# Eight attention steps with their division by the row sum moved behind the values product

## The chip, the cores and the metric

The kernel runs on one core of one Trainium2 chip. The metric is the device time of one execution in microseconds (us), the median of three runs. The engines are TensorE (PE in the profile, PEld for its weight loads), VectorE (DVE), ScalarE (ACT), GpSimd (POOL) and SyncE (SP), which here issues nearly all DMAs. Each engine works through its own instructions in the order in which the program emits them, as the rows of the trace below show it; engines wait for one another by semaphores.

## The reference

Attention over 8 batches, 8 heads, 576 tokens and a head width of 64, in float32, with a threshold on the scores; its output is rearranged to 4608 tokens of width 512 and goes through a two-layer feed-forward block with ELU.

```python
scores = (q @ k.T) / sqrt(64)
thresh = max(scores) - tau
scores = where(scores >= thresh, scores, -1e9) - max(scores)
attn = exp(scores)
attn = attn / (sum(attn) + 1e-9)
o = attn @ v                      # (8, 8, 576, 64)
x = o.transpose(0, 2, 1, 3).reshape(4608, 512)
h = x @ w_in                      # (4608, 2048)
g = where(h > 0, h, exp(min(h, 0)) - 1)
out = g @ w_out                   # (4608, 512)
```

## The kernel before, in words

The unit of attention is a *pair*: two heads of one batch, so 4 pairs for each of 8 batches. A pair has five *steps*, one for each tile of 128 query tokens (tiles 0 to 3) and one for the last 64 tokens of both heads. The list `steps` sets their order. It begins with tiles 0 and 1 of pairs 0, 1, 2, 3; these are steps 0 to 7, step n being tile n % 2 of pair n // 2. Tiles 2, 3 and the tail of batch 0 are steps 8 to 19, and the later batches follow.

A step holds 128 query rows in the partitions and 576 keys for each of two heads along the free axis. Its jobs, all made in `early_tasks`, are named here as in the code, with "n/h" for step and head:

- `sc`: TensorE writes the scores into PSUM (L673). `max` (VectorE, L730) takes the row maximum, `th` the threshold.
- `exp` and `mask`: either ScalarE's exponential (L768) and VectorE's compare-and-multiply (L775), or two activations on ScalarE (L753, L759), write the weights `w`, with their row sums accumulated beside them.
- `su` and `rec`: the sum and its reciprocal `rs`, 128x2 (L783 or L720, and L789).
- `norm` n/h: `w` is multiplied by `rs`, 128x576 for each head, on GpSimd (L726), ScalarE (L714) or VectorE (L709), as the tables ACT_NORM and NORM_DVE say. In steps 0 to 7 eleven of the sixteen are on GpSimd, four on ScalarE, one (4/0) on VectorE.
- `part` n/x and `put` n/x, x from 0 to 2: TensorE turns 4, 4 and 1 blocks of 128x128 of `w` into a PSUM tile `rt` (L792), and ScalarE, or VectorE where PUT_DVE says so, copies it to the tile `wTa` or `wTb` (L808).
- `val` (pair, part): TensorE multiplies the values by the turned weights of two steps, into a PSUM tile `pv` (L925 and L930, 18 recorded instructions). `out` (pair, part): the result, 128 channels by 256 tokens, is copied to `xt`, the input of the feed-forward block (L1060).

The PSUM tiles `rt` and `pv` share one pool of two buffers, `psum["t"]`. `room_for("t", release)` keeps a list of two releases: before a third tile is taken, the oldest one's release (its `put` or `out`) is emitted.

Beside the steps the first 60 us hold the conversion of the feed-forward weights from their stored form, in pieces of 128x512: `rest` (L485 or L505), `shift` (L492 or L494), `add` (L500, GpSimd), `sign` (L510, ScalarE) and `end` (L518, VectorE). Pairs are prepared by `prep` (VectorE, L577 and L590), `scale` (L582 or L584) and `copy` (GpSimd, L629).

The order of all this is written by hand: each job has a due time, shifted by the table MOVED; jobs are emitted by due time, and `do` emits what a job needs ahead of it.

```python
def do(x):
    job = made[x]
    if not job[4]:
        job[4] = True
        for y in job[3]:
            if y:
                do(y)
        job[2]()
...
def room_for(pool, release):
    while len(taken[pool]) >= 2:
        taken[pool].popleft()()
    taken[pool].append(release)
```

From step 10 on (after `switch`, at some 50 us) the feed-forward block of earlier tokens is woven in between the steps.

Of the kernel before, what the change touches and what calls it, by code (L numbers as in the profile page):

```python
# [10 lines left out]
FP32 = mybir.dt.float32  # L11
# [4 lines left out]
ALU = mybir.AluOpType  # L16
# [352 lines left out]
def kernel(  # L369
# [10 lines left out]
    nc = tc.nc  # L380
    PSUM = bass.MemoryType.PSUM
    P = 128
    B, H, S, D = q.shape
    DM, DF = moe_w_in.shape
    NC = S // P
    MAIN = NC * P
# [5 lines left out]
    KJ = DM // P  # L392
    NFT = DF // P
    NPAIR = H // 2
# [8 lines left out]
    xpool = ctx.enter_context(tc.tile_pool(name="xpool", bufs=2))  # L403
# [13 lines left out]
    wstage = early.enter_context(tc.tile_pool(name="wstage", bufs=2))  # L417
    wpool = [wstage]
    banks = ExitStack()
    psum = {"t": banks.enter_context(tc.tile_pool(name="ps_t", bufs=2, space=PSUM))}  # L420
# [214 lines left out]
    wTs, xts, open_steps, turns = {}, {}, {}, {}  # L635
# [80 lines left out]
    def total_act(pr, i, hs):  # L716
# [2 lines left out]
        st["summed"] = True  # L719
        nc.scalar.activation(st["su"][:, cs], st["sm"][:, cs, 0], AF.Identity, bias=st["sm"][:, 0, 1:2])  # L720

    def normalize(pr, i, hs):
        st = open_steps[pr, i]
        for h in hs:
            wv = st["w"][:, h * S : (h + 1) * S]
            nc.gpsimd.tensor_scalar(wv, wv, st["rs"][:, h : h + 1], 1.0, ALU.mult, ALU.mult)  # L726
# [64 lines left out]
    def transpose(dst, src):  # L791
        nc.tensor.matmul(dst, src, idents[-1], is_transpose=True, skip_group_check=True)  # L792
# [104 lines left out]
    def fetch(pr, i):  # L897
# [11 lines left out]
        else:  # L909
# [2 lines left out]
                back.rearrange("k (a b) n -> k a b n", b=2),  # L912
            )

    def values(pr, part, pv=None):
        b, j = divmod(pr, NPAIR)
        vm, vd = (raws[pr][x] for x in ("vm", "vd"))
        wT = wTs.pop((pr, part))
        if b not in xts:
            xts[b] = xpool.tile([P, KJ, MAIN], FP32, name="xt")  # L920
        n = wT.shape[1] * T
        if pv is None:
            pv = psum["t"].tile([P, 512], FP32, name="pv", tag="rt")
        watch = on_banks if wide else lambda *a: None
        watch(nc.tensor.matmul(pv[:, :n], vd, wT[:, :, NC], start=True, stop=False, skip_group_check=True), pv[:, :n])  # L925
        for c in range(NC):
            for h in range(2):
                g0, g1 = (2 * h, 2 * h + 10) if part else (0, 2 * NT)
                o = pv[h * D : (h + 1) * D, g0 * T : g1 * T]
                watch(nc.tensor.matmul(o, vm[:, h, c], wT[:, g0:g1, h * (NC + 1) + c], start=False, stop=(c == NC - 1),  # L930
                                       skip_group_check=True), o)
        return lambda: values_out(pr, part, pv)

    wide, turned_by = [], []
# [120 lines left out]
    def values_out(pr, part, pv):  # L1055
        b, j = divmod(pr, NPAIR)
        q0, n = TAIL * part, (3 if part else 2) * NT * T
        watch = on_banks if wide else lambda *a: None
        o = pv[:, q0 : q0 + 2 * P]
        watch(nc.scalar.copy(xts[b][:, j, part * 2 * P : (part + 1) * 2 * P], o), o)  # L1060
        if part:
            xs = opool.tile([P, TAIL], FP32, name="xs", bufs=2)
            for h in range(2):
                r = slice(h * D, (h + 1) * D)
                o = pv[r, h * (n - TAIL) : h * (n - TAIL) + TAIL]
                watch(nc.scalar.copy(xs[r], o), o)  # L1066
            nc.sync.dma_start(xtail[j, :, b * TAIL : (b + 1) * TAIL], xs)
            pairs.pop(pr), raws.pop(pr)
# [106 lines left out]
    steps = [(pr, i) for pr in range(NP) for i in ((0, 1, NC, 2, 3) if pr >= JOINED else range(NB))]  # L1175
    steps[:per_seq] = [(pr, i) for x in ((0, 1), (2, 3, NC)) for pr in range(NPAIR) for i in x]
    LATE = 10

    def behind(pr, i):
        if i in (1, NB - 1):  # L1180
# [114 lines left out]
    def task(x, t, key, f, *needed):  # L1295
        each = "_".join(map(str, x)) if isinstance(x, tuple) else x
        made[x] = [t + (MOVED.get(key, 0.0) if key else 0.0) + MOVED.get(each, 0.0), len(made), f, needed, False]
# [10 lines that stand above are left out]
    def early_tasks():  # L1308
# [5 lines left out]
# [4 lines that stand above are left out]
# [54 lines left out]
        for pr in range(1, NPAIR + 6):  # L1372
            old = ("sc", number[pr - 2, NC]) if pr > 1 else None
            own = pr < NPAIR
            for x, name in enumerate("qk"):
                n = 2 * pr - 2 + x if own else number[pr - 1, 2 + x]
                k, late_ = kind(n), n >= LATE
# [26 lines left out]
                m = number[pr, 2] if own and not x else n  # L1404
# [15 lines left out]
        for i, (n, x) in enumerate(slots):  # L1420
            late_, k, t = n >= LATE, f"{kind(n)}{x}", begin[n]
            m, y = slots[max(i - 4, 0)]
# [47 lines left out]
        for n in range(MIDDLE):  # L1470
# [16 lines left out]
            for h in hs:  # L1487
                task(("max", n, h), at_(0.2 + 0.5 * h, 1.8 + 0.6 * h, 0.8 + 0.5 * h), f"max{h}{k}", lambda pr=pr, i=i, h=h: max_of(pr, i, h), ("sc", n))
                back = ("turned", n - (2 if last_ else WBUFS)) if n >= WBUFS else None
                t_exp, t_th, t_mask = (at_(0.3 + 0.7 * h, 2.0 + 0.6 * h, 1.0 + 0.5 * h), at_(0.4 + 0.7 * h, 2.2 + 0.6 * h, 1.1 + 0.5 * h),  # L1490
                                       at_(2.0 + 1.6 * h, 5.6 + 0.1 * h, 4.0 + 0.1 * h))
                if (n, h) in MASK_ACT:
                    task(("exp", n, h), t_exp, f"exp{h}{k}", lambda pr=pr, i=i, h=h: sink_of(pr, i, h), ("th", n, h), back, "late" if last_ else None)
                    task(("th", n, h), t_th, f"th{h}{k}", lambda pr=pr, i=i, h=h: pivot_of(pr, i, h), ("max", n, h))
                    task(("mask", n, h), t_mask, f"mask{h}{k}", lambda pr=pr, i=i, h=h: raise_of(pr, i, h), ("exp", n, h))
                else:
                    task(("exp", n, h), t_exp, f"exp{h}{k}", lambda pr=pr, i=i, h=h: exp_of(pr, i, h),
                         ("max", n, h), exps[-1] if exps else None, ("mask", *exps[-2][1:]) if len(exps) > 1 else None)
                    task(("th", n, h), t_th, f"th{h}{k}", lambda pr=pr, i=i, h=h: bound_of(pr, i, h), ("max", n, h))
                    exps.append(("exp", n, h))  # L1500
                    task(("mask", n, h), t_mask, f"mask{h}{k}", lambda pr=pr, i=i, h=h: mask_of(pr, i, h), ("exp", n, h), ("th", n, h),
                         ("mask", n, 0) if h and (n, 0) not in MASK_ACT else back, "late" if last_ else None)
                scaled = normalize_act if (n, h) in ACT_NORM else normalize_dve if (n, h) in NORM_DVE else normalize_pool
                norm = lambda pr=pr, i=i, h=h, f=scaled: f(pr, i, h)
                task(("norm", n, h), at_(5.0 + 0.8 * h, 6.2 + 0.1 * h, 5.4 + 0.1 * h), f"norm{h}{k}", norm, ("rec", n))
            task(("su", n), at_(3.8, 5.8, 4.4), f"su{k}", lambda pr=pr, i=i, hs=hs, f=total_act if n in SU_ACT else total_of: f(pr, i, hs), *[("mask", n, h) for h in hs])
            task(("rec", n), at_(3.8, 5.8, 4.4), f"rec{k}", lambda pr=pr, i=i, hs=hs: reciprocal_of(pr, i, hs), ("su", n))
# [10 lines left out]
            else:  # L1518
# [11 lines left out]
                m = n + 1  # L1530
# [14 lines left out]
            if i in (1, NC) and n < MIDDLE - 4:  # L1545
                got = []
                mine_ = [number[pr, x] for x in ((0, 1) if i == 1 else (2, 3, NC))]

                def run_values(pr=pr, part=part, got=got):
                    room_for("t", lambda: do(("out", pr, part)))  # L1550
                    got.append(values(pr, part))

                def run_out(pr=pr, part=part, got=got):
                    got[0]()
                    if (pr, part) == (NPAIR - 1, 0):
                        push_ffn(0)
                    elif (pr, part) == (NPAIR - 1, 1):
                        push_ffn(1)

                m = n + 2  # L1560
                t_val, t_out = (begin[m] + 4.0, begin[m] + 6.2) if m < LATE else (begin[m] + 0.4, begin[m] + 3.3)
                if n < per_seq:
                    t_val, t_out = begin[n + 1] + 4.2, begin[n + 2] + 1.5
                    if n >= LATE:
                        t_val, t_out = begin[n + 1] + 5.6, begin[n + 1] + 6.8
                elif any(m in SQUARES for m in mine_):
                    t_val, t_out = begin[n + 3] + 5.7, begin[n + 3] + 5.8
                elif SWITCH + 1 >= m >= SWITCH:
                    t_val, t_out = t_val - 8.0, t_out - 8.0
                task(("val", pr, part), t_val, f"val{k}", run_values, *[("landed", m) for m in mine_], ("v", pr))  # L1570
                task(("out", pr, part), t_out, f"out{k}", run_out, ("val", pr, part), ("out", pr, 0) if part else None)
            if n == 0:
                task("idle", t + 2.1, None, lambda: idle(16))
            if n >= SWITCH:
# [777 lines left out]
```

## Time and profile before

| what | value |
|---|---|
| median of three runs | 1259.22 us (1258.13 to 1260.99) |
| the profiled execution | 1259.32 us |
| its span in the profile | 1257.5 us |
| busy: PE, DVE, ACT, POOL | 99%, 83%, 51%, 58% of the span |
| granted TensorE clock | 1.00 |
| `norm` on GpSimd (L726) in the first 70 us | 14 of 798 ns |
| `norm` on ScalarE (L714) in the first 70 us | 8 of 773 ns |
| `out` (L1060) from `pv` | 16 of 365 ns |

The busy shares are averages over the whole span. The changed work lies in its first 50 us of 1257.5, where a step passes through all engines, so this stretch is read by itself: its busy time by engine, the chain of waits, and the timeline of each engine.

### The profile page before, as it was taken

Reading aid. Unit: us, or ns where it says so; the run is one execution under the profiler, and the core shown is the slowest. Engines: PE = TensorE matmul, PEld = TensorE weight load, DVE = VectorE, ACT = ScalarE, POOL = GpSimd, SP = SyncE. Lnnn points to the kernel's source line nnn. Section 1 sums busy time; section 2 is a strip of 40 time slices with the busy share of each in tenths; the row PEclk is TensorE's granted clock in tenths of the full one; section 3 lists DMA queues with packets and bytes.
Section 4 is the critical chain, followed back from the end, with each engine's and each line's share of the span. In section 5 each row is a group of like instructions: output and inputs, shape, how many; then the busy total and the mean of one; then the engine's idle time right before and its main releaser. Section 6 shows DMA issues by size and latency. Waiting matters only on the chain.

```text
span 1257.5 us, 21116 instructions
## 1 busy us (share of the span) xinstructions
PE 1243.9 (99%) x6598; PEld 957.0 (76%) x6598; DVE 1040.3 (83%) x2199; ACT 635.2 (51%) x1331; POOL 727.1 (58%) x1061
## 2 busy tenths in 40 slices
PE   8999999999999999999999999999999999999998
PEld 6676576467878787888778787878788887788886
DVE  7888778789798988898889879898889876776983
ACT  7989776664352526253534435252625353465330
POOL 4778655687475847666576747584766655122000
PEclk9999999999999999999999999999999999999999
DMA  7557688998889898998989998999889885000001
GB/s 134 151 177 177 177 244 234 260 248 216 239 239 266 245 240 224 241 263 228 252 206 253 237 231 231 256 257 240 228 238 262 221 241 175 20 1 1 1 34 34
DMA packets 325551, 245.74 MB, mean 195 GB/s; under 512 B 209216, under 2 KB 289984, under 8 KB 325440
## 3 DMA queue, kind: packets, MB, share of 16 engines
q1 hardware_dynamic: 323264, 243.65, 72.2%
q8 instruction: 52, 0.85, 0.3%
q10 hardware_dynamic: 2176, 0.75, 0.2%
q14 instruction: 59, 0.48, 0.1%
HBM read 154.53 MB, written 89.78 MB: 194 GB/s over the span
## 4 chain that ended last, share of the span: by engine, by line
PE 90%; DVE 3%; DMA 2%; ACT 2%; issue 1%; SPq 1%; POOL 1%; DVEq 0%; ACTq 0%; POOLq 0%
PE f L1678 23%; PE f L1818 22%; PE sc L977 8%; PE sc L1050 7%; PE f L2278 7%; PE f L2203 5%; PE f L1102 4%; PE sc L673 3%; PE f L1154 3%; PE f L2216 2%; PE pv L930 2%; PE rt L792 1%; PE sc L1042 1%; PE sc L1037 1%; DMA there<-x 1%
## 5 line engine op out<-in xcount | busy, mean ns | idle before, releaser
L984 DVE TENSOR_REDUCE mx<-sc 128x1 f32<-128x576 f32 x207 | 148.3, 750 | 28.5 <-PE sc L977 24.6
L726 POOL TENSOR_SCALAR w<-w,rs 128x576 f32<-128x576 f32 x144 | 115.8, 813 | 70.0 <-DVE rs L789 69.8
L1004 ACT ACTIVATE w<-sc,mx 128x576 f32<-128x576 f32 x113 | 81.5, 740 | 116.0 <-DVE mx L984 98.7
L868 DVE STREAM_TRANSPOSE x<-w 128x512 f32<-128x512 f32 (+1 forms) x153 | 108.9, 744 | 15.3 <-POOL w L726 11.3
L996 POOL TENSOR_SCALAR th<-mx,ntau 128x2 f32<-128x2 f32 (+1 forms) x114 | 33.8, 297 | 133.3 <-DVE mx L984 133.3
L977 PE MATMUL sc<-kT,qT 64*128 64x448 f32 (+4 forms) x736 | 103.4, 416 | 0.2 <-ACT xs L1066 0.2
L977 PEld LDWEIGHTS sc<-kT,qT 64*128 64x128 f32 x736 | 81.0, 186 | 25.1 <-issue 16.5
L1011 DVE SCALAR_TENSOR_TENSOR w<-sc,th,w 128x576 f32<-128x576 f32 x113 | 88.2, 811 | 9.4 <-ACT w L1004 9.2
L1678 PE MATMUL f<-xt,sw 128*128 128x256 f32 x384 | 93.8, 386 | 1.8 <-DVE g L1700 1.8
L1678 PE MATMUL f<-xt,w_in 128*128 128x256 f32 x384 | 92.2, 382 | 0.0
L1818 PE MATMUL f<-w_out,s 128*128 128x256 f32 x384 | 92.0, 382 | 0.1
L1818 PE MATMUL f<-w_out,g 128*128 128x256 f32 x384 | 92.0, 382 | 0.0
L1678 PE MATMUL f<-x,w_in 128*128 128x256 f32 x384 | 90.9, 379 | 0.0
L1818 PE MATMUL f<-t,s 128*128 128x256 f32 x384 | 90.8, 379 | 0.0
L726 POOL TENSOR_SCALAR e<-e,rs 128x576 f32<-128x576 f32 x91 | 67.1, 741 | 35.6 <-DVE rs L789 34.2
L1678 PEld LDWEIGHTS f<-xt,sw 128*128 128x128 f32 x384 | 69.4, 189 | 18.6 <-issue 4.8
L1678 PEld LDWEIGHTS f<-xt,w_in 128*128 128x128 f32 x384 | 71.7, 190 | 12.7 <-ACT w L1692 2.2
L1818 PEld LDWEIGHTS f<-w_out,g 128*128 128x128 f32 x384 | 72.0, 190 | 12.4 <-issue 3.1
L1818 PEld LDWEIGHTS f<-w_out,s 128*128 128x128 f32 x384 | 71.9, 190 | 12.4 <-issue 2.5
L1678 PEld LDWEIGHTS f<-x,w_in 128*128 128x128 f32 x384 | 72.8, 190 | 10.5 <-ACT s L1692 0.6
L1818 PEld LDWEIGHTS f<-t,s 128*128 128x128 f32 x384 | 72.8, 190 | 10.3 <-POOL s L1765 0.4
L1765 POOL TENSOR_TENSOR s<-g 128x256 f32<-128x256 f32 x96 | 74.9, 785 | 7.9 <-DVE g L1728 7.5
(316 smaller groups left out, 3103.5 us busy)
## 6 DMA issues: line engine op xcount, KB each, us to landing
there<-x SPq DMA_DIRECT2D x444, 144.0 KB, 3.5
wTb<-there SPq DMA_DIRECT2D x58, 576.0 KB, 6.5
wTa<-there SPq DMA_DIRECT2D x53, 576.0 KB, 5.0
sw<-win_sums SPq DMA_DIRECT2D x46, 384.0 KB, 4.9
t<-wout_sums SPq DMA_DIRECT2D x33, 512.0 KB, 6.2
qm<-in_q_dram SPq DMA_DIRECT2D x124, 72.0 KB, 4.9
wst<-in_moe_w_in_dram SPq DMA_DIRECT2D x16, 512.0 KB, 4.4
vm<-in_v_dram SPq DMA_DIRECT2D x64, 128.0 KB, 3.9
```

Source lines behind the costliest of these rows:

```text
L726: nc.gpsimd.tensor_scalar(wv, wv, st["rs"][:, h : h + 1], 1.0, ALU.mult, ALU.mult)
L868: nc.vector.transpose(x[:, :, c0 : c0 + nc_], src.rearrange("p (c g n) -> p g c n", c=nc_, n=T))
L977: on_banks(nc.tensor.matmul(o, qT[r, i * P : (i + 1) * P], kT[r, k0 : k0 + n], start=True, stop=True, skip_group_check=True), o)
L984: on_banks(nc.vector.tensor_reduce(st["mx"][:, h : h + 1], st["sc", h], axis=AX.XY if i == NC else AX.X, op=ALU.max, negate=True), st["sc" ...
L1004: on_banks(nc.scalar.activation(st["e", h], st["sc", h], AF.Exp, bias=st["mx"][:, h : h + 1]), st["sc", h])
L1011: on_banks(nc.vector.scalar_tensor_tensor(st["e", h], st["sc", h], st["th"][:, h : h + 1], st["e", h], ALU.is_ge, ALU.mult, accum_out=st[" ...
L1050: on_banks(nc.tensor.matmul(o, vm[:, h, c], parts[part][:, g0:g1, h * (NC + 1) + c], start=False, stop=(c == NC - 1), skip_group_check=Tru ...
L1678: nc.tensor.matmul(loc["banks"][place], left[:, j], right[:, j], start=(begins and j == 0), stop=(j == 1), skip_group_check=True)
L1765: engine.tensor_tensor(o, x, y, op)
L1818: nc.tensor.matmul(place(m), lhs, rhs, start=(begins and v == 0), stop=(v == RU - 1), skip_group_check=True)
L2203: nc.tensor.matmul(o, w.rearrange("p (j f) -> p j f", j=KJ)[:, j], m, start=(j == 0 and x == 0), stop=(j == KJ - 1 and x == 1), skip_group ...
L2278: nc.tensor.matmul(banks8[2 * i + x // 2], h[:, tok], w, start=(f == 0 and x != 1), stop=(f == NFT - 1 and x != 0), skip_group_check=True)
```

## The change

For steps 0 to 7 (tiles 0 and 1 of pairs 0 to 3) the weights are turned and multiplied by the values without having been divided by their row sums; the division is made on the product. As the product has channels in its partitions and tokens along the free axis, the factors have to be turned too:

- `norm` n/0 becomes `widen`: GpSimd writes `rs` (128x2) 64 times side by side, a 128x128 tile for both heads. `norm` n/1 becomes nothing. So 16 multiplications of 128x576 go, and 8 copies of 128x128 come.
- `spread` (pair): TensorE turns the two wide tiles of a pair into a PSUM tile `rt` from `psum["t"]`. It is needed by `val` (pair, 0), so it is emitted just ahead of it.
- `scales` (pair): ScalarE copies that, 128x256, to the place in `xt` where the values of this pair will stand. It is emitted when `room_for` calls for its release, or by `out` at the latest.
- `out` (pair, 0) for these pairs: instead of ScalarE's copy VectorE multiplies `pv` by what stands in `xt`, into `xt`.

The new jobs have a due time of 9000, so their place in the order follows from who needs them. Nothing else in the tables is altered.

```diff
+    def widen(pr, i):
+        st = open_steps[pr, i]
+        st["wide"] = wstage.tile([P, 2, D], FP32, name="rsd", bufs=3)
+        nc.gpsimd.tensor_copy(st["wide"], st["rs"].unsqueeze(2).broadcast_to([P, 2, D]))
...
+    def spread(pr):
+        rt = psum["t"].tile([P, 512], FP32, name="rt", tag="rt")
+        for i in range(2):
+            transpose(rt[:, i * P : (i + 1) * P], open_steps[pr, i]["wide"].rearrange("p h d -> p (h d)"))
+        return rt
+
+    def keep_spread(pr, rt):
+        b, j = divmod(pr, NPAIR)
+        if b not in xts:
+            xts[b] = xpool.tile([P, KJ, MAIN], FP32, name="xt")
+        scales[pr] = xts[b][:, j, : 2 * P]
+        nc.scalar.copy(scales[pr], rt[:, : 2 * P])
...
-        watch(nc.scalar.copy(xts[b][:, j, part * 2 * P : (part + 1) * 2 * P], o), o)
+        if (pr, part) in UNSCALED:
+            nc.vector.tensor_tensor(xts[b][:, j, : 2 * P], o, scales.pop(pr), ALU.mult)
+        else:
+            watch(nc.scalar.copy(xts[b][:, j, part * 2 * P : (part + 1) * 2 * P], o), o)
...
+    UNSCALED, LAST = [(pr, 0) for pr in range(NPAIR)], 9000.0
...
+                if (pr, int(i >= 2)) in UNSCALED:
+                    norm = (lambda: None) if h else lambda pr=pr, i=i: widen(pr, i)
                 task(("norm", n, h), at_(5.0 + 0.8 * h, 6.2 + 0.1 * h, 5.4 + 0.1 * h), f"norm{h}{k}", norm, ("rec", n))
...
-                task(("val", pr, part), t_val, f"val{k}", run_values, *[("landed", m) for m in mine_], ("v", pr))
-                task(("out", pr, part), t_out, f"out{k}", run_out, ("val", pr, part), ("out", pr, 0) if part else None)
+                if (pr, part) in UNSCALED:
+                    got_spread = []
+
+                    def run_spread(pr=pr, got_spread=got_spread):
+                        room_for("t", lambda: do(("scales", pr)))
+                        got_spread.append(spread(pr))
+
+                    task(("spread", pr), LAST, None, run_spread, *[("rec", m) for m in mine_])
+                    task(("scales", pr), LAST, None, lambda pr=pr, got_spread=got_spread: keep_spread(pr, got_spread[0]),
+                         ("spread", pr), ("out", pr - 1, 0) if pr else None)
+                task(("val", pr, part), t_val, f"val{k}", run_values, *[("landed", m) for m in mine_], ("v", pr),
+                     ("spread", pr) if (pr, part) in UNSCALED else None)
+                task(("out", pr, part), t_out, f"out{k}", run_out, ("val", pr, part),
+                     ("out", pr, 0) if part else ("scales", pr) if (pr, 0) in UNSCALED else None)
```

More of the change, by code (lines that the diff above doesn't have):

```diff
@@ L913, in fetch @@
             )
+    scales = {}
+    def spread(pr):
[9 more added lines that the diff above has]
+        nc.scalar.copy(scales[pr], rt[:, : 2 * P])
     def values(pr, part, pv=None):
```

## The prediction, on record before the result

> **What bounds the kernel now.** The page first. TensorE is busy nearly throughout, but this is an average, and the change touches only the first 50 us. So the second view is the busy time of each engine in stretches of 10 us (columns: us of PE, PEld, DVE, ACT, POOL; clock; DMA).
>
> ```profile
> PE 1243.9 (99%) x6598; PEld 957.0 (76%) x6598; DVE 1040.3 (83%) x2199; ACT 635.2 (51%) x1331; POOL 727.1 (58%) x1061
> ```
>
> ```profile
> 10.00:20.00 10.00, 8.61 (x56) 6.06 (x54) 7.59 (x19) 9.86 (x20) 6.74 (x10) 1.00 0.83 163
> ...
> 30.00:40.00 10.00, 9.30 (x72) 6.22 (x73) 9.39 (x23) 8.77 (x17) 5.25 (x11) 1.00 0.87 223
> ```
>
> GpSimd has the most room here, VectorE and ScalarE little. No engine alone sets the pace: the third view, the chain of waits (start, us, what), hops from one to the next. From 62.8 us on it is nearly all TensorE, without gaps until 212 us, so what the first 63 us lose or gain is kept to the end, unless a later stall takes it up.
>
> ```profile
> 28.30 0.53 DVE w L709
> ...
> 29.59 0.43 PE pv L925 x2
> ...
> 32.49 1.22 PE sc L673 x8
> 33.71 0.75 DVE mx L730
> ...
> 34.54 0.62 ACT e L768
> ...
> 36.48 0.33 PE rt L792
> 36.80 1.17 PE sc L673 x8
> ```
>
> Of the sixteen multiplications that go, only two places lie on this chain: steps 0/0 and 0/1 on GpSimd (a piece of 1.33 us at 12.63) and step 4/0 on VectorE (0.53 us at 28.30, above). The rest of the chain is work that stays. The fourth view, the timeline around 33 us, shows what `out` of pair 1 releases:
>
> ```profile
> 33.19 0.39 ACT L1060 COPY xt<-pv 128x256 f32<-128x256 f32 x1
> ...
> 33.59 0.14 PEld L792 LDWEIGHTS rt<-ident,w 128*128 128x128 f32 x1 [0.39 <-ACT xt L1060]
> ...
> 33.69 1.42 DVE L730 TENSOR_REDUCE mx<-sc 128x1 f32<-128x576 f32 x2 [0.36 <-PE sc L673]
> ...
> 33.95 0.27 ACT L808 COPY wTa<-rt 128x128 f32<-128x128 f32 x1 [0.37 <-PE rt L792]
> 34.54 1.41 ACT L768 ACTIVATE e<-sc,mx 128x576 f32<-128x576 f32 x2 [0.32 <-DVE mx L730]
> ...
> 35.03 0.69 DVE L518 SCALAR_TENSOR_TENSOR w_in<-wtop,wst 128x512 f32<-128x512 f32 x1
> ```
>
> ScalarE's copy (L1060) frees a PSUM buffer; TensorE's `part` 4/2 waits for just that (the bracket), ScalarE's `put` 4/2 waits for `part` 4/2, and `exp` 6/0, on the chain, stands behind it in ScalarE's queue.
>
> **The change, part by part.** Durations are those of the profiled execution, 1259.32 us with a span of 1257.5; it lies 0.1 us above the median.
>
> Work as such: GpSimd loses 11 x 0.80 = 8.8 us and gains 8 widenings. No row shows one; the 64x64 copy (L629) takes 0.235 us, the 128x128 select that makes `ident` 0.29, the 128x576 multiplication 0.80. I take 0.3, the 128x128 row, with 0.24 and 0.80 as ends; GpSimd's idle time (4.75 us of 10 between 30 and 40) hides either. ScalarE loses 4 x 0.77 = 3.1 us; its four copies of 128x256 change place (0.365 us each, L1060). VectorE loses 0.52 and gains four multiplications of 128x256 with one operand in PSUM, 0.42 us each by L1700 (422 ns, same shape and places). TensorE gains 8 turns of 0.15 us (four take 0.59 to 0.63, L792). None of these sums decides; the places do. I followed the jobs in the order in which `do` emits them, which the trace bears out, engine by engine.
>
> *Pair 0 (to 25 us).* `widen` 0 in place of two multiplications lets GpSimd's `scale` of pair 1 (14.07) start some 0.7 us sooner, but `sc` 2 also needs the buffer that `mask` 1/0 on VectorE frees at 14.61 (`sc` 2 began at 14.87), so about 0.5 us is won. ScalarE loses `norm` 1/1 and keeps this lead to the `put`s at 18.8; then 0.3 us of turns go in ahead of `val` 0, VectorE's `out` 0 (0.42) pushes `mask` 3/1, and `sc` 4 waits for `mask` 3/0 as before (end 22.8). By `exp` 4/0 (25.44), where ScalarE sets the pace, I find no difference. Bounds: 0.5 us gained, 0.4 us lost. Taken: 0.
>
> *Pair 1, ahead of `val`.* `part` 4/0 no longer waits for `norm` 4/0: it starts at 28.5 instead of 28.96. But the turns take one of the two PSUM buffers, so `val` 1 now needs the buffer of `part` 4/0 itself, and hence its `put` (0.59, L808): 28.5 + 0.63 + 0.05 + 0.59 + 0.05 = 29.85 against 29.59. The turns run while that copy does. +0.26 us; bounds 0 and +0.5.
>
> *Pair 1, `out`.* This is the large one. `out` 1 keeps its place in the emitted order: `max` 6/0, `max` 6/1, `end` 0, `put` 4/1, `out` 1, `part` 4/2, `put` 4/2, `exp` 6/0, `mask` 6/0. On ScalarE it had nothing of these but `put` 4/1 ahead of it and ran at 33.19. On VectorE it stands behind both maxima, which need `sc` 6, and behind `end` 0. Those end at 35.72, with the 0.26 above at 35.98. Then `out` 1 to 36.40, `part` 4/2 (0.33) to 36.75, `put` 4/2 (0.27) to 37.03, and only then `exp` 6/0, before at 34.54: +2.49, of which 0.26 is counted already. Behind the waiting TensorE instruction stand nine idle turns and `part` 5/0 and 5/1 (2.2 us, done by 38.9, where `put` 5/0 then is, so no more is lost); behind ScalarE's, both exponentials. +2.23 us; bounds 1.8 (part of the 0.69 us of `end` 0 could run in VectorE's gap of 0.36 us before the maxima) and 2.6.
>
> *Pair 2.* The two turns go between `sc` 7 and `val` 2, both on the chain (36.80, 37.98), with their buffer long free: +0.30 us; bounds 0 and 0.4. `scales` 2 (0.36) ahead of `out` 2 (0.42) ahead of `max` 8/0 costs VectorE 0.6 us more than before, but `exp` 8/0 waits on ScalarE for `put` 6/0 anyway: +0.05; bounds 0 and 0.5.
>
> *Pair 3.* The turns run while TensorE waits for `put` 7/2 (0.35 us at 47.29): nothing. `scales` 3 goes into ScalarE's queue between `norm` 8/0 and `exp` 9/0 (47.44 and 48.44, both on the chain): +0.36; `out` 3 delays `mask` 9/0 by as much on the parallel branch to `su` 9, so the two don't add up. Bounds 0.1 and 0.6.
>
> Sum: 0 + 0.26 + 2.23 + 0.30 + 0.05 + 0.36 = 3.2 us. What is left up to 62.8 us is GpSimd's `norm` 9 (51.47) and, behind it in the same queues, the conversion of weights: no changed work, and it starts when `rec` 9 is done. So 1259.3 + 3.2 = 1262.5, or 1262.4 from the median. The terms' bounds together give 1260.7 to 1263.8; not all ends can fall together, and I take 1261.0 to 1264.0 as this case's own range.
>
> **The rivals.** *Taken up again (same).* GpSimd is freed of 3.7 us between 33 and 46 (steps 5 to 7), and the chain passes through its conversions at 54.39 (0.88, L505) and 55.34 (1.31, L500). If these could run ahead of `norm` 9, up to 2.2 us would come back: 1260.3. Against it: they stand behind `norm` 9 in GpSimd's queue. The same end would come from transfers after 212 us that the chain waits for (4.42 us for `vd` at 225.76), if they don't shift with the rest.
>
> *The division was the brake (faster).* If `out` 1 did get through on VectorE before `max` 6/0 (its gap there is 0.36 us, the multiplication 0.42), the big term is gone, and with it the 0.26. The pieces on the chain then count: 1.33 - 0.3 at step 0, 0.53 + 0.14 at step 4, and 2.2 at the conversions, less 0.7 for pairs 2 and 3: 1259.3 - 3.2 = 1256.1. It decides at one point: which comes first on VectorE, the first multiplication of pair 1 or L518 of piece 0. The order of emission speaks against it.
>
> *TensorE's clock (slower still).* Between `sc` 6 (end 34.0) and `part` 4/2 (36.4) TensorE would stand for 2.4 us, more than any stop between 12 and 60 us now. If the clock then halved for the 3.4 us after it, 1.7 us of work would be lost, of the 4 us on the chain from 36.48 to 40.48: 1264.1. For now the granted clock is 1.00 in every stretch, also at 8 to 10 us, where TensorE is busy for 0.88 of 2 us.
> The Trainium skill (TensorE: Matmul & The Clock Gate, Part 1) has the clock halved after an idle window of about 3.4 us, free-running; by that rule 2.4 us is too short. No trace here shows a fall of the clock inside the work.
>
> That the change fails to do what it says I leave at nothing: each new job is needed by one that must run.
>
> **How the numbers follow.** Forecast 0.62, taken up again 0.19, faster 0.12, clock 0.07. About 0.2% (2.5 us) is what a measurement of this kernel tells from no change; the forecast is only just over it, so a tenth of its chance (0.06) goes to "same". Slower: 0.56 + 0.07 = 0.63; same: 0.19 + 0.06 = 0.25; faster: 0.12. The range reaches down over the rival that ends near 1260 and up over the clock: 1258.5 to 1264.8, which leaves out the faster case and little else.
>
> **What would show it.** Right: VectorE's multiplication of pair 1 at about 36 us, right after L518; TensorE's single turn of step 4 ended by "DVE xt", after a stop of over 2 us; `exp` 6/0 at about 37.0, `sc` 7 at about 39.3, `sc` 8 at about 43.2; and the stretch that now begins with `sc` at 62.82 beginning near 66. The clock 1.00 throughout. Wrong: `exp` 6/0 within 1 us of 34.54, or a shift at 37 us that is smaller at 63 or at 300 us; then the queue orders, or the keeping of a delay, were read wrongly.

## The result, and the profile after

The changed kernel takes 1261.47 us (median; 1259.99 to 1262.39), beside 1259.14 us for the kernel before in the same session. The ratio is 1.0017 with an interval of 1.0010 to 1.0024: slower by 2.1 us (1.3 to 3.0) by that ratio. The prediction said 1262.4 us, slower, by 3.2 us. The sign and nearly the size were right; the road to them was not. The term that made up 2.23 of the 3.2 us did not occur at all.

The profiled execution takes 1261.05 us with a span of 1259.3, against 1259.32 and 1257.5 before. First the page's busy line, then the busy time by stretches (us of PE, PEld, DVE, ACT, POOL; clock; DMA), which answer to the ones shown of before.

```profile
PE 1245.9 (99%) x6606; PEld 958.5 (76%) x6606; DVE 1041.9 (83%) x2202; ACT 633.4 (50%) x1327; POOL 720.9 (57%) x1058
```

```profile
10.00:20.00 10.00, 9.04 (x62) 6.69 (x62) 8.29 (x20) 9.85 (x22) 5.13 (x9) 1.00 0.93 185
...
30.00:40.00 10.00, 9.46 (x71) 6.16 (x71) 8.85 (x22) 7.13 (x14) 4.72 (x12) 1.00 0.75 200
```

GpSimd is relieved by 6.2 us in all (727.1 to 720.9) and ScalarE by 1.8, VectorE gains 1.6 and TensorE 2.0. The clock stays at 1.00. The averages don't say why the time grew; the chain of waits around the multiplication of pair 1 says more (start, us, what):

```profile
28.55 0.60 ACT wTa L813
29.14 0.04 issue
29.19 0.70 PE pv L945 x2
29.89 1.88 PE pv L950 x16
31.77 0.59 PE rt L797 x4
32.35 1.22 PE sc L673 x8
33.57 1.40 DVE mx L735 x2
34.98 0.23 DVE w_in L518
35.21 0.28 issue
35.49 0.38 DVE xt L1081
```

`val` of pair 1 stands behind `put` 4/0 at 28.55 as predicted, and the multiplication (L1081) stands behind both maxima and behind L518, at 35.49, also as predicted (36 us). What it holds up is another thing than predicted. The timeline around it (start, us, engine, line, what; in brackets the idle time before and what ended it):

```profile
33.45 0.33 PE L797 MATMUL rt<-ident,w 128*128 128x128 f32 x1
...
33.82 0.27 ACT L813 COPY wTa<-rt 128x128 f32<-128x128 f32 x1 [0.84 <-PE rt L797]
...
34.41 1.41 ACT L773 ACTIVATE e<-sc,mx 128x576 f32<-128x576 f32 x2 [0.32 <-DVE mx L735]
...
35.49 0.42 DVE L1081 TENSOR_TENSOR xt<-pv,xt 128x256 f32<-128x256 f32 x1
...
35.97 0.82 PE L797 MATMUL rt<-ident,w 128*128 128x128 f32 x5 [0.19 <-DVE xt L1081]
```

The single turn of `part` 4/2 ran at 33.45, two microseconds before the multiplication that it was to wait for, and `exp` 6/0 began at 34.41 (34.54 before). It is `part` 5/1, at 35.97, that waited for the multiplication, and only for 0.19 us.

To find where the time went, the same instruction is looked up in both traces, in order, and its two starts, counted from the start of each span, are subtracted. The first work, at 5 to 15 us, is already 0.12 us late in this profile:

| stretch or instruction | after minus before, us |
|---|---|
| TensorE, 15 to 25 us | -0.60 |
| `val` 1, second part (29.82; 29.95) | -0.13 |
| `exp` 6/0 (34.41; 34.54) | -0.13 |
| `sc` 8 (40.57; 40.41) | +0.16 |
| `norm` 8/0 on ScalarE (47.80; 47.44) | +0.36 |
| `exp` 9/0 (49.06; 48.44) | +0.62 |
| `su` 9 (51.97; 50.93) | +1.04 |
| all engines, 62 to 210 us | +0.85 |
| the end of the work | +1.72 |

So 0.85 - 0.12 = 0.73 us are lost in the first 63 us, mostly between 47 and 52 us, and the rest of the loss comes much later, in places that the change doesn't touch. Beyond 210 us this table has to be read with care, as it rests on one execution of each kernel: between 212 and 300 us the shift falls back to 0.40, and there the profile before has a stop of TensorE of 1.37 us of its own (269.95 to 271.32).

Where 0.36 becomes 1.04, the timeline after shows `scales` 3 (L933) ahead of the exponential, and `out` 3 (L1081) with VectorE standing idle ahead of it:

```profile
48.48 0.35 ACT L933 COPY xt<-rt 128x256 f32<-128x256 f32 x1
...
49.06 0.83 ACT L773 ACTIVATE e<-sc,nb,keep 128x576 f32<-128x576 f32 x1
...
50.37 0.42 DVE L1081 TENSOR_TENSOR xt<-pv,xt 128x256 f32<-128x256 f32 x1 [0.98 <-PE pv L950]
...
51.04 0.81 DVE L780 SCALAR_TENSOR_TENSOR w<-sc,th,e 128x576 f32<-128x576 f32 x1
51.28 1.30 POOL L500 TENSOR_TENSOR wtop<-wtop,wst 128x512 int32<-128x512 int32 x1 [1.95 <-DVE wtop L494]
...
52.01 1.21 PE L673 MATMUL sc<-x,qd 128*128 128x288 f32 x4 [1.17 <-DVE w L780]
```

In the kernel before, the mask and the scores of step 10 stand here:

```profile
49.46 0.82 DVE L775 SCALAR_TENSOR_TENSOR w<-sc,th,e 128x576 f32<-128x576 f32 x1
...
50.44 1.21 PE L673 MATMUL sc<-x,qd 128*128 128x288 f32 x4
```

VectorE waits 0.98 us for `val` 3 and holds up all that is queued behind: `mask` 9/0 (L780, 51.04 instead of 49.46), the shift of a weight piece (L494) with GpSimd's `add`, and through the mask the scores of step 10 on TensorE, 1.57 us late here.

### The profile page after: what moved, and what is told of

Same layout as the page of the kernel before. It is cut to its first block, busy times and chain, and to the rows that moved or that the text cites. A ratio compares the mean times of both kernels' runs of the same rounds, so it can differ in the third digit from the quotient of the medians.

```text
span 1259.3 us, 21124 instructions
## 1 busy us (share of the span) xinstructions
PE 1245.9 (99%) x6606; PEld 958.5 (76%) x6606; DVE 1041.9 (83%) x2202; ACT 633.4 (50%) x1327; POOL 720.9 (57%) x1058
## 4 chain that ended last, share of the span: by engine, by line
PE 87%; DMA 4%; DVE 4%; SPq 1%; ACT 1%; issue 1%; POOL 0%; DVEq 0%; ACTq 0%; POOLq 0%
PE f L1856 22%; PE f L1716 19%; PE sc L1070 7%; PE sc L997 7%; PE f L2316 7%; PE f L2241 5%; PE f L1125 5%; PE sc L673 3%; PE f L1177 3%; PE f L2254 2%; PE pv L950 2%; PE rt L797 2%; DMA there<-x 2%; PE sc L1062 1%; DVE x L873 1%
## 5 line engine op out<-in xcount | busy, mean ns | idle before, releaser
L731 POOL TENSOR_SCALAR w<-w,rs 128x576 f32<-128x576 f32 x133 | 107.4, 816 | 63.2 <-DVE rs L794 63.2
L997 PE MATMUL sc<-kT,qT 64*128 64x448 f32 (+3 forms) x736 | 103.6, 417 | 0.2 <-ACT xs L1089 0.2
```

What stands on the lines that cost most here:

```text
L997: on_banks(nc.tensor.matmul(o, qT[r, i * P : (i + 1) * P], kT[r, k0 : k0 + n], start=True, stop=True, skip_group_check=True), o)
```

## The experiments

The theories, as the result leaves them. *Places*: the change loses where its new jobs stand in the queues, above all `out` 3 and `scales` 3. *Amount*: it loses by the work that it adds. *Brake*: the sixteen multiplications by the reciprocal limited the kernel, and taking them away gains. And beside these the question why the prediction's large term is missing: *wrong dependency* (the price was right, but `part` 4/2 doesn't wait for that multiplication), or *taken up* (such a delay would vanish further on).

"Late at 63 us" below is measured as above: TensorE's starts between 62 and 100 us against the kernel before, less the same at 5 to 15 us.

**e1_removal.** The kernel before with no division at all in steps 0 to 7, and nothing put in its place:

```diff
+                if n < 8:
+                    norm = lambda: None
```

> Leaves out the division by the row sum in steps 0 to 7 (first 256 tokens of batch 0) and adds nothing. Theory 'places': the two pieces on the chain go, so pair 0 gives 0.6 us (as seen at 15 to 25 us in the changed kernel) and step 4/0 another 0.5: start of the stretch at 62.8 us 1.1 us earlier, and the time 1.1 us shorter. Rival 'the division was the brake': GpSimd's conversions move ahead too, 3 us shorter. Rival 'hidden': less than 0.3 us at 62.8.

1258.62 us, ratio 1.0000 (0.9991 to 1.0009); at 63 us it is 0.5 us early. The kernel leaves the division out, so its output is not that of the reference. The brake is refuted: all sixteen multiplications together are worth about half a microsecond by 63 us, less than half of the 1.1 us expected by *places*, and nothing that can be measured at the end. There was little to win, whatever the replacement had cost.

**e2_pair0.** The changed kernel with the new way in pair 0 alone:

```diff
-    UNSCALED, LAST = [(pr, 0) for pr in range(NPAIR)], 9000.0
+    UNSCALED, LAST = [(0, 0)], 9000.0
```

> The change for pair 0 alone (steps 0 and 1). Theory 'places': 0.6 us earlier at 25 us, and nothing after it takes that back: 0.6 us earlier at 62.8 and 0.6 shorter in all. Rival 'taken up': back to the old times by 35 us, the time unchanged. Rival 'any other start of the later stages costs at the transfers': earlier by 0.6 at 62.8 but up to 1 us longer in all.

1258.98 us, ratio 1.0002 (0.9993 to 1.0011). TensorE is 0.75 us early at 15 to 20 us, level from 25 to 35 us, and then 0.36 us late; net of the start 0.40 at 63 us. The gain at step 0, which the prediction put at 0.5 us, is there, and it is given back as the prediction had it. That later steps then lose 0.36 was not expected: *places* had 0.6 us gained at 63 us. In this profile the 0.36 us arise at one place, where `exp` 6/1 begins (35.56) 0.26 us after `exp` 6/0 with no other engine named as the cause. No other profile has this gap, so it isn't shown to come of the change.

**e3_delay.** The kernel before with one additional copy on ScalarE ahead of `exp` 9/0, which is then overwritten:

```diff
+        if (pr, i, h) == (0, 3, 0):
+            nc.scalar.copy(e, st[h][:, :, :HALF])
```

> The kernel before with one ScalarE copy of 128x576 more (0.83 us) ahead of the exponential of step 9/0 at 48.4 us, overwritten at once: a bare delay, nothing else. It starts the stretch at 62.8 us about 0.8 us later, as the changed kernel does (0.85). Theory 'kept': the time grows by 0.8 us. Theory 'grows': a later start of that size costs more at the waits for transfers after 212 us, and the time grows by about 2.3 us as in the changed kernel.

1259.23 us, ratio 1.0006 (0.9997 to 1.0014); 0.57 us late at 63 us. In the profile the copy holds ScalarE for 0.65 us (48.14 to 48.79). A delay at this place is on the path, and nine tenths of it are still there at 63 us. The total can't be told from that of the kernel before.

**e4_out3_late.** The changed kernel with `out` 3 behind `rec` 9 on VectorE:

```diff
+                if (pr, part) == (NPAIR - 1, 0):
+                    MOVED[f"out{k}"] = 0.0
+                    t_out = 84.5 - MOVED.get("out_3_0", 0.0)
```

> The changed kernel with the multiplication of pair 3 emitted behind the reciprocal of step 9 instead of ahead of the compare of step 9/0. Theory 'places': the compare runs 0.8 us sooner, the sum of step 9 follows ScalarE (0.6 us late instead of 1.0), and the stretch at 62.8 us begins 0.3 to 0.5 us after that of before instead of 0.85: 0.4 us shorter than the changed kernel. Rival: the delay comes from ScalarE's copy of the factors of pair 3 alone, no difference to the changed kernel.

1259.90 us, ratio 1.0012 (1.0003 to 1.0020); 0.48 us late at 63 us instead of 0.73. VectorE's timeline now has the mask first and `out` 3 out of the way:

```profile
49.88 0.82 DVE L780 SCALAR_TENSOR_TENSOR w<-sc,th,e 128x576 f32<-128x576 f32 x1 [0.28 <-ACT e L773]
...
51.70 0.40 DVE L1081 TENSOR_TENSOR xt<-pv,xt 128x256 f32<-128x256 f32 x1
```

So 0.25 us of the loss at 63 us is the place of `out` 3. The totals of the two kernels can't be told apart.

**f1_changed_again.** The changed kernel, unaltered, in another session.

> The changed kernel once more, unaltered, beside the next three. If its loss after the first 63 us (0.7 us late there net of the start, 2.1 us at the end) belongs to the change, the ratio is again 1.0017 and the second profile again shows a growth at 300 to 700 us of about 1.3 us. If the growth is the chance of one profile and one session, the ratio comes nearer 1.0006 (0.7 us of 1259) and the second profile's growth lies elsewhere or is missing.

1260.83 us, ratio 1.0018 (1.0009 to 1.0027); 0.80 us late at 63 us. The loss repeats, and it is more than those 0.8 us.

**f2_placed.** The changed kernel with its new jobs put elsewhere. The work is the same, save that VectorE makes the copy of the factors of pair 3:

```diff
+        for x, t, needed in ((("spread", 1), 36.5, ()), (("scales", 2), 59.5, (("sc", 7),)), (("spread", 3), 68.5, (("norm", 7, 0),)),
+                             (("scales", 3), 9000.0, (("max", 8, 1),)), (("out", 1, 0), 44.5, ()),
+                             (("out", 2, 0), 61.5, (("mask", 7, 0),)), (("out", 3, 0), 84.5, ())):
+            made[x][0], made[x][3] = t, (*needed, *made[x][3])
...
-        nc.scalar.copy(scales[pr], rt[:, : 2 * P])
+        (nc.vector.tensor_copy if pr == 3 else nc.scalar.copy)(scales[pr], rt[:, : 2 * P])
```

> The changed kernel with its new jobs put elsewhere: the turns of pairs 1 and 3 earlier, the copy of factors 2 behind the scores of step 7, that of pair 3 on VectorE, the multiplications of pairs 1, 2 and 3 at other places among VectorE's jobs. If the late stretch at 50 us (multiplication of pair 3, copy of its factors) is what the change loses, the same scores that were 0.7 us late at 63 us come at most 0.1 us late or up to 0.4 us early, and the time is that of the kernel before, ratio 0.9995 to 1.0003. If it is the amount of work added (VectorE, TensorE) and not its place, the ratio stays at 1.0012 or more.

1259.01 us, ratio 1.0002 (0.9993 to 1.0011); 0.18 us late at 63 us, a little more than the 0.1 expected. Places it is, not amount: with the same 8 turns, 8 widenings, 4 copies and 4 multiplications no loss is left that can be told from the kernel before. The places were altered all at once; `out` 3 alone was tried in e4. It is not faster, and e1 says why it can't be by much.

**f3_changed_pinned.** The changed kernel, with `part` 4/2 turned into the very PSUM tile `pv` that the multiplication of pair 1 reads. The order of each engine's instructions stays as it is; this wait is new. It is the dependency that the prediction had assumed.

```diff
-            pv = psum["t"].tile([P, 512], FP32, name="pv", tag="rt")
+            pv = psum["t"].tile([P, 512], FP32, name="pv", tag="rt"); raws["pv", pr, part] = pv
...
-        def room():
-            rt = psum["t"].tile([P, NC, P], FP32, name="rt", tag="rt")
+        def room(own=False):
+            rt = raws["pv", 1, 0].rearrange("p (c n) -> p c n", n=P) if own else psum["t"].tile([P, NC, P], FP32, name="rt", tag="rt")
...
-            rt = room()
+            rt = room(own=(pr, i, c0) == (2, 0, NC))
```

> The changed kernel with one thing altered: the last part of step 4 (part 4/2) is turned into the very PSUM tile that the multiplication of pair 1 reads, so that it must wait for that multiplication, as the prediction had it. The prediction's large term: part 4/2 at about 35.9, exponential 6/0 at 36.4 to 37.0 in place of 34.4, the scores of step 7 2.0 to 2.5 us later than in the changed kernel, and the time 2.2 us over it (1.8 to 2.6), ratio to before 1.0030 to 1.0036. Rival, the delay would be taken up on the way to 63 us (GpSimd and VectorE have room): exponential 6/0 late as above, but the time within 0.7 us of the changed kernel's.

1262.98 us, ratio 1.0035 (1.0022 to 1.0047), 2.15 us over f1 beside it. The timeline:

```profile
35.64 0.42 DVE L1081 TENSOR_TENSOR xt<-pv,xt 128x256 f32<-128x256 f32 x1
...
36.12 0.33 PE L797 MATMUL pv<-ident,w 128*128 128x128 f32 x1 [2.44 <-DVE xt L1081]
36.17 1.68 PEld L797 LDWEIGHTS rt<-ident 128*128 128x128 f32 x9
36.28 1.97 PE L797 MATMUL rt<-ident 128*128 128x128 f32 x9
36.48 0.27 ACT L813 COPY wTa<-pv 128x128 f32<-128x128 f32 x1 [3.36 <-PE pv L797]
36.64 1.38 ACT L773 ACTIVATE e<-sc,mx 128x576 f32<-128x576 f32 x2
```

Step for step the prediction's walk, with a stop of TensorE of 2.44 us ended by "DVE xt", `put` 4/2 and then `exp` 6/0 at 36.64, which is 2.23 us later than in the changed kernel. But the scores of step 7 are at 40.05, 3.34 us later than in the changed kernel (36.71), not 2.2. The row of f3, then that of the changed kernel:

```profile
40.05 1.24 PE L673 MATMUL sc<-kT,qT 64*128 64x288 f32 x8
```

```profile
36.71 1.24 PE L673 MATMUL sc<-kT,qT 64*128 64x288 f32 x8
```

The stretches say why (after the five engines come the granted clock, the DMA share and GB/s):

```profile
33.00:36.00 3.00, 0.67 (x6) 0.19 (x2) 2.38 (x5) 0.12 (x1) 1.33 (x4) 1.00 0.81 169
36.00:37.00 1.00, 0.89 (x6) 0.89 (x7) 0.06 (x1) 0.52 (x2) 0.86 (x1) 0.72 0.95 238
37.00:39.00 2.00, 2.00 (x11) 2.00 (x10) 1.50 (x5) 1.02 (x2) 0.00 (x0) 0.50 0.88 252
39.00:40.00 1.00, 1.00 (x6) 0.71 (x4) 0.69 (x5) 0.59 (x2) 0.14 (x1) 0.58 0.60 246
40.00:41.00 1.00, 1.00 (x9) 0.69 (x8) 0.00 (x0) 1.00 (x3) 0.15 (x1) 1.00 0.04 16
```

The granted clock falls to 0.50 behind the stop: it is the prediction's third rival, which could only come up together with the large term.

At 63 us f3 is 4.15 us late, 3.35 more than f1, but the two medians lie 2.15 us apart. That the total meets the 2.2 us expected is therefore luck in part: the clock added 1 us that the expectation lacked, and about as much of the lateness doesn't show in the total. Where that went isn't shown; with five executions of f3, spread over 2.7 us, it can be chance.

**f4_before_pinned.** The same pinning in the kernel before, where ScalarE's copy is the reader of that tile.

> The kernel before with the same single alteration: part 4/2 is turned into the PSUM tile from which ScalarE copies the values of pair 1. ScalarE's copy comes right behind put 4/1, which part 4/2 waits for now: no more than 0.4 us at exponential 6/0, the time within 0.4 us of the kernel before, ratio 0.9997 to 1.0004. If the alteration itself costs something (the buffer that part 5/0 then has to wait for), that shows here, and is to be taken off the run beside it.

1258.41 us, ratio 0.9997 (0.9988 to 1.0005); level with before at 63 us (-0.05). The pinning by itself costs nothing, so what f3 costs is the late multiplication, with the stop of TensorE that it brings.

**g2_pinned_again** and **g3_pinned_busy**. The first is f3 unaltered; the second adds 16 idle turns ahead of `part` 4/2, into the PSUM tile that `put` 4/1 has read by then:

```diff
+            if (pr, i) == (2, 0) and c0:
+                raws["busy"] = rt if c0 > NC else raws["busy"]
+                for _ in range(16 if c0 == NC else 0):
+                    transpose(raws["busy"][:, 0], ident)
```

> The changed kernel with part 4/2 in the PSUM tile of the multiplication of pair 1, once more and unaltered. In its first profile the granted clock fell to 0.50 from 36.3 to 39.6 us, behind a stop of TensorE of 2.44 us, and the scores of step 7 were 3.3 us late, while the median was 2.15 us over the changed kernel. If the clock falls behind this stop in every execution, it shows again at the same place. If it depends on where the stop falls, this profile may have 1.00 throughout, with the scores of step 7 2.2 us late and an execution of some 1263.

> The same pinned kernel with 16 idle turns of 128x128 on TensorE ahead of part 4/2 (some 2.1 us of work into a buffer that is free by then), so that TensorE does not stand while it waits. If the fall of the clock comes of the stop, the clock is 1.00 here, part 4/2 still waits for the multiplication (about 36.1), exponential 6/0 is at 36.6 as in the pinned kernel, and the scores of step 7 are at 38.9 in place of 40.05; the time is 2.0 to 2.3 us over the changed kernel, ratio to before about 1.0033, and 0 to 1.1 us under the pinned one. If the clock falls for another reason, it falls here too.

g2: 1263.01 us, ratio 1.0038 (1.0024 to 1.0051); the clock again 0.50 from 37 to 39 us, the scores of step 7 again at 40.05. g3: 1262.04 us, ratio 1.0029 (1.0019 to 1.0040). The stretches and TensorE's timeline of g3:

```profile
36.00:37.00 1.00, 0.67 (x6) 0.67 (x7) 0.28 (x1) 0.30 (x2) 1.00 (x2) 1.00 0.95 299
37.00:39.00 2.00, 1.75 (x15) 1.42 (x13) 1.28 (x3) 2.00 (x4) 0.08 (x1) 1.00 0.76 250
```

```profile
33.82 1.97 PE L797 MATMUL rt<-ident 128*128 128x128 f32 x16
36.34 0.33 PE L797 MATMUL pv<-ident,w 128*128 128x128 f32 x1 [0.55 <-DVE xt L1085]
...
39.03 1.24 PE L673 MATMUL sc<-kT,qT 64*128 64x288 f32 x8
```

With TensorE kept at work the same wait still ends with the multiplication, the clock is 1.00 throughout, and the scores of step 7 come at 39.03, 2.3 us later than in the changed kernel. The stop, not the wait, brings the clock down, and that costs 1.0 us at step 7. The difference of the two medians is 1263.01 - 1262.04 = 0.97 us, of the expected size, though the two intervals overlap.

**g1_delay_more** and **h1_placed_delay**. These ask whether the loss after 63 us is a consequence of being late. Two copies on ScalarE ahead of `exp` 9/0, in the kernel before and in f2:

```diff
+        if (pr, i, h) == (0, 3, 0):
+            nc.scalar.copy(e, st[h][:, :, :HALF])
+            nc.scalar.copy(e[:, 0], st[h][:, 0, :HALF])
```

> The kernel before with a pure delay: two extra copies on ScalarE (128x576 and 128x288) ahead of exponential 9/0, so that everything from there on is about as late as in the changed kernel (0.57 us came of the one copy; about 0.9 us is expected at 63 us). If being late by so much at 63 us is by itself what makes transfers late further on, the time is 1.8 us or more over the kernel before, ratio 1.0014 to 1.002. If a delay is kept and no more, the ratio is 1.0004 to 1.001, and what the changed kernel loses beyond 0.8 us has another cause.

> The kernel with the jobs placed elsewhere (ratio 1.0002, 0.1 us late at 63 us) plus the pure delay of the two ScalarE copies, so that it is about as late at 63 us as the changed kernel, with the same work as that. A delay that is kept and no more gives 1.0 us over the placed kernel, ratio 1.0007 to 1.0011, and no steps of 0.3 us at 545 and 825 us in its profile. If lateness together with the changed kernel's program brings those steps, the ratio is 1.0015 or more and both steps are in the profile.

g1: 1259.25 us, ratio 1.0009 (1.0000 to 1.0018), 0.92 us late at 63 us. This is what a delay that is kept and no more would give, though the interval reaches into the other expectation (1.0014 and over). h1: 1260.76 us, ratio 1.0016 (1.0007 to 1.0025), 1.03 us late at 63 us, which leaves its total between the two expectations: the ratio fits the second, the profile, without the steps at 545 and 825 us, the first. What these steps are, the chain of waits shows, of f1 and then of f4 at the same time:

```profile
821.90 2.81 PE f L1716 x13
824.71 1.00 PE sc L997 x3
825.71 0.14 SPq L1274
825.85 0.04 issue
825.90 5.66 DMA wTb<-there
831.56 0.80 DVE e L1031 x3
```

```profile
821.85 0.65 PE f L1678 x3
822.49 2.14 PE sc L977 x12
824.63 8.40 PE f L1678 x38
```

In f4 (and in the kernel before) this stretch is TensorE's alone; in f1 a transfer of turned weights ends last, and 0.37 us are lost. In the first profile of the changed kernel the chain passes through other transfers at both places. Against f4 a like step of 0.34 to 0.37 us stands at 545 us, and both are in all five profiles of kernels in which `out` 3 keeps its place (the changed one twice, f3, g2, g3), however late they are at 63 us (0.7 to 4.2 us). In f2, h1, g1 and e4 neither is there; e4 has a step of 1.1 us near 560 us instead, f2 one of 0.6 near 695 us. The first profile of the changed kernel has one of 0.5 near 560 us beside the two.

## Why the prediction came out, point by point

*What bounds the kernel.* Right in its main claim: a delay made in the first 63 us is still there at 63 us (nine tenths of it in e3), and no engine's sum decides (e1, f2). That such a delay is kept to the end was not shown to better than about 1 us: of f3's 3.35 us over f1 the medians show 2.15.

*The prices of the new work* held: a widening took 0.29 us (0.3 said), a multiplication 0.42 (0.42), a copy of factors 0.35 to 0.40 (0.36), two turns 0.41 to 0.44, of which 0.27 pass before the next matmul begins (0.30).

*Pair 0.* Taken as 0 within -0.5 and +0.4; measured -0.72 net of the start at 15 to 25 us. The lead is real, larger than the bound, and at `exp` 4/0, where the prediction found no difference, the changed kernel is still 0.60 us ahead. In e2, where pair 0 alone is changed, the lead is gone by 25 us, as said.

*Pair 1, ahead of `val`.* Said +0.26; of the lead 0.47 us are lost there (-0.60 to -0.13), for the reason given: `val` 1 waits for `put` 4/0. (The terms of this sum make 29.82, not the 29.85 written there; it matters little.)

*Pair 1, `out`.* The step that failed. The place of the multiplication on VectorE was right to half a microsecond; that `part` 4/2 waits for it was wrong. The prediction took this from "[0.39 <-ACT xt L1060]", which stood on the weight load of that turn. But the bracket names the event that came last before it, and the turn itself began at 33.59 as the scores of step 6 ended, with no wait of its own: it follows the first matmul of those scores by 1.17 us, and so it does in the changed kernel (32.28 and 33.45), where the multiplication is two microseconds away. The built programs give `part` 4/2 the PSUM buffer of `put` 4/1 in both kernels, not that of `out` 1: the list in `room_for` says only what must be emitted before a third tile is taken, and not which of the two buffers the tile then gets. +2.23 became 0, and the multiplication at 35.49 cost a wait of 0.19 us at `part` 5/1, of which 0.11 arrived at `sc` 7. f3 shows that the price was right for the dependency assumed, as far as `exp` 6/0: 2.23 us there.

*Pair 2.* Said +0.30 and +0.05. Measured +0.18 at `sc` 8 (from -0.02 at `sc` 7 to +0.16) and +0.20 more by `norm` 8/0: `out` 2 delays the maximum of step 8, and the wait on ScalarE for `put` 6/0 does not hide all of it.

*Pair 3.* Said +0.36, with `out` 3 in parallel to `scales` 3, so that the two don't add up. They do: +0.26 at `exp` 9/0 by `scales` 3, and another 0.42 by `su` 9, of which e4 takes back 0.25 by 63 us when `out` 3 is moved.

*The sum.* Net of the start: -0.72 by 25 us, +0.47 at `val` 1, +0.11 at `sc` 7, +0.18, +0.20, +0.26 and +0.42 as above, and 0.19 taken back between `su` 9 and 63 us: 0.73 us in place of 3.2. The end came near the forecast because about 1 us more was lost later, in part at transfers, for which the sum had no term: two wrong sizes of opposite sign, and so luck. The bounds of the terms were added up wrongly at the upper end: they make 5.0 us, so 1264.3, not 1263.8; the forecast doesn't rest on it. By the prediction's own test, `exp` 6/0 within 1 us of 34.54, the queue orders and waits were read wrongly.

*The rivals.* "Taken up again" didn't hold, nor did the brake. The brake's condition, the early multiplication, was not met; the large term was gone all the same, but the gains that it listed came to 0.5 us (e1) instead of over 3. The fall of TensorE's clock had no occasion in the changed kernel, as the stop was missing. In f3, where the stop is there, it halved as the rival had it and cost 1.0 us, not 1.7.

*What stays open.* Why the changed kernel loses 2.1 to 2.3 us in all when it is 0.7 to 0.8 us late at 63 us. Lateness alone gave 1.0009 in g1, but the interval reaches 1.0018, and h1, as late with the changed kernel's work, has 1.0016. The two steps at transfers go with the place of `out` 3 in every profile, but how something at 50 us reaches 545 us isn't shown, and they make up only 0.7 us; h1 had the loss in its ratio without them. Nor can single profiles settle it: between 62 and 300 us the profile before falls 1.1 us behind that of f4, whose kernel differs in the place of one tile alone, and this is about as much as is to be explained.

## What to carry to other kernels

A releaser in brackets tells what came last, not what was needed; before a delay is priced along a buffer, look up which buffer the waiting instruction really writes, since a pool of two need not alternate. Price a removal first by how much sooner the next steps would come without the work at all: here sixteen multiplications with 11.8 us of engine time were worth half a microsecond. And work that moves into another engine's queue costs by what stands behind it there: `out` 3 ahead of the mask cost 0.25 us at 63 us (e4).

## What the runs showed of the hardware

A stop of TensorE of 2.44 us was enough to halve its clock: f3 and g2 have 0.50 from 37 to 39 us, and the averages of the neighbouring slices (0.72 and 0.58 in f3) put the half-speed stretch at about 36.4 to 39.8 us, an estimate of 3.4 us. The fall came some 0.3 us after TensorE had gone back to work, and 1.0 us was lost by it. TensorE's stop of 1.17 us ahead of 52.01 in the profile after left it at 1.00, and so did one of 1.37 us ahead of 271.32 in the profile before. No profile has a stop of between 1.37 and 2.44 us from one matmul to the next, so where the limit lies is not shown. With 16 turns in the stop (g3) the clock stayed at 1.00.
The Trainium skill (TensorE: Matmul & The Clock Gate, Part 1) gives an idle window of about 3.4 us before the clock is halved, and as long a stretch of work before it is whole again. The second agrees with the 3.4 us here; the first doesn't, in both profiles with the stop, and the measurement decides: the stop need not be as long as the window. In the 3 us from 33 to 36 TensorE was still busy for 0.67 us in f3.
